# Attention's scores, products and exponentials in another order within a step

## The chip, the cores and the metric

The kernel runs on one NeuronCore of a Trainium2 chip. The time is that of one execution on the device, in microseconds (us). The kernel before took 920.6 us as the median of three runs (917.02 to 921.53).

Four engines matter here, each working through its own list of instructions in order: TensorE (PE, matrix products), ScalarE (ACT, tanh and exp), VectorE (DVE, sums, copies and transposes) and SyncE (SP, which issues most of the transfers). They wait for one another by semaphores. An instruction that waits holds up all that stand behind it on its engine.

## The reference

Softmax attention with capped scores comes first; its result feeds a layer of eight experts in which every expert takes 448 of the 3584 tokens.

```python
# q, k, v: (batch 8, heads 12, seq 448, head_dim 64), cap 30
scores = scale * np.matmul(q, k.transpose(0, 1, 3, 2))
scores = cap * np.tanh(scores / cap)
attn = np.exp(scores - scores.max(-1, keepdims=True))
attn = attn / (attn.sum(-1, keepdims=True) + 1e-09)
x = np.matmul(attn, v)          # then as 3584 tokens x 768
# logits = x @ w_gate; tokens go to experts in the order of their logits
out[mask] = np.maximum(x[mask] @ w1[e], 0) @ w2[e]
```

## The kernel before

Attention runs in 24 steps (the loop over `g`), three to a batch. I call the three m=0, m=1 and m=2, after the variable `m`. One step handles four heads.

**Scores.** Step g computes its scores in seven rounds, `qk(g,0)` to `qk(g,6)`. A round is four matmuls (64x64 weights, 448 columns) into a score tile `psS` of two PSUM banks, and then a tanh over 128x896 on ScalarE (line 145), which I call T0 to T6. Only two `psS` tiles exist, so the matmuls of a round wait until the tanh two rounds earlier has emptied its tile.

**Exponentials.** The seven rounds form groups: rounds 0 and 1, rounds 2 and 3, rounds 4 to 6. When a group's last tanh is issued, one exp over the whole group follows it on ScalarE (line 149): E0 and E1 over 128x1792, E2 over 128x2688. So ScalarE's list in a step is T0 T1 E0 T2 T3 E1 T4 T5 T6 E2.

**Products.** The exponentials of step g are multiplied with `v` one step later. `avq(g-1,j,x)` (line 177) is eight 64x64 matmuls that use rounds 2j and 2j+1 of the step before; j=3 uses round 6. They come as `x=0` with j=0 to 2 and as `x=1` with j=0 to 3, all into two `psA` tiles, which VectorE copies to `xT` (line 187) at the end of the step.

**Other work on TensorE** comes between `qk(g,1)` and the first products (place A), and between the x=0 and the x=1 part (place B). What stands there depends on m and on the batch. For batches 2 to 5 (steps 6 to 17): in m=0 two `xt` transposes at A and two at B (line 37); in m=1 two `xt` at A and sums and gates at B (`rnd`, line 194); in m=2 three lists of `rnd` at A and the transposes of the logits at B (line 209). Step 5, the m=2 step of batch 1, has the same `rnd` at A. From step 18 on A holds nothing in m=0, one list of `rnd` in m=1, the logit transposes in m=2.

**VectorE** adds the exponentials up into `es` (line 153), transposes the next step's `k` and `q` (line 125), and does the small work on logits. **SyncE** loads `k`, `q` and `v` up to three steps ahead.

The order on TensorE, ScalarE, VectorE and SyncE is the order in which the Python code issues the instructions; no planner changes it in this part. The rest of the kernel (routing, and the experts' two layers, some 580 us) follows attention and isn't touched.

Of the kernel before, what the change touches and what calls it, by code (L numbers as in the profile page):

```python
# [7 lines left out]
AF=mybir.ActivationFunctionType; ALU=mybir.AluOpType; AX=mybir.AxisListType  # L8
# [9 lines left out]
def attention(nc, tc, c1, xp, pM, q, k, v, cap, w_gate, xs, L1, ident, on_logits, on_turn, NDEF, xd, setup, mark):  # L18
# [33 lines left out]
    with ExitStack() as ctx:  # L52
# [11 lines left out]
        def load(g,part,lo=0,hi=HG,first=False):  # L64
            if g>=N: return
            b,m=divmod(g,NQ)
            h0=4*m
            if part==2:
                z=nat.tile([128,3,2*HG,D],F32,name="nv",bufs=5); zh=nat.tile([128,HG,D],F32,name="nvh",bufs=5)
                nats[g,2]=(z,zh)  # L70
                vv=v[b,h0:h0+4,0:384].rearrange("h (j p) d -> j p h d",j=3)
                for j in range(3): nc.sync.dma_start(z[:,j],vv[j])
                for o in range(2):
                    for t in range(2):
                        w=64*(1-o)
                        nc.sync.dma_start(zh[w:w+64,t],v[b,h0+2*t+o,384:448])
                return
            if lo==0: nats[g,part]=nat.tile([128,HG*NB,32],F32,name="kq"[part])
            z=nats[g,part]
            src=(k,q)[part]  # L80
            for t in range(2):
                for a in range(2):
                    w=(2*t+a)*32
                    (nc.scalar if first and a else nc.sync).dma_start(z[w:w+32,lo*NB:hi*NB,:],src[b,h0+2*t+lo:h0+2*t+hi,:,a*32:a*32+32].rearrange("h (k s) d -> s (h k) d",s=32))  # L84
# [6 lines left out]
        capt=c1.tile([128,1],F32,name="capt")  # L91
# [18 lines left out]
        def gates():  # L110
            for g in range(NQ):
                for t in range(2):
                    nc.sync.dma_start(wgs[t*64:t*64+64,2*g:2*g+2,:],w_gate[(4*g+2*t)*D:(4*g+2*t+2)*D].rearrange("(m d) e -> d m e",d=D))
            for bi,(g,p,hs) in enumerate(blk):
                for h in hs:
                    l=loc[h][1]; hp=slice(h%2*64,h%2*64+64)
                    nc.gpsimd.tensor_copy(gw[hp,bi,3+8*l:11+8*l],wgs[hp,h//2,:])
# [4 lines left out]
        def tr(g,part,lo=0,hi=HG):  # L122
            if g>=N: return
            if lo==0: tks[g,part]=tp.tile([128,HG,S],F32,name="t"+"kq"[part])
            nc.vector.transpose(tks[g,part].rearrange("p m s -> p (m s)")[:,lo*S:hi*S],nats[g,part][:,lo*NB:hi*NB,:].rearrange("p k d -> p (k d)"))
        GRP=((0,1),(2,3),(4,5,6)); LOC={r:(gi,n) for gi,rs in enumerate(GRP) for n,r in enumerate(rs)}
        def ev(g,r):
            gi,n=LOC[r]
            return eh[g,gi][:,n]
        ex=lambda g,o,j: ev(g,3*o+j if g==0 else 2*j+o)  # L130
        def qk(g,r):
            gi,n=LOC[r]
            if n==0: eh[g,gi]=ep.tile([128,len(GRP[gi]),2,S],F32,name=f"e{gi}")
            ps=pS.tile([128,2,512],F32,name="psS")
            if r<6:
                o,u=divmod(r,3) if g==0 else divmod(r,2)[::-1]
                for h in range(2):
                    hp=slice(h*64,h*64+64)
                    for c in range(2): nc.tensor.matmul(ps[c*64:c*64+64,h,:S],tks[g,0][hp,o,u*128+c*64:u*128+c*64+64],tks[g,1][hp,o,:],start=True,stop=True)  # L139
            else:  # L140
                for o in range(2):
                    for h in range(2):
                        hp=slice(h*64,h*64+64); w=64*(1-o)
                        nc.tensor.matmul(ps[w:w+64,h,:S],tks[g,0][hp,o,384:448],tks[g,1][hp,o,:],start=True,stop=True)  # L144
            nc.scalar.activation(ev(g,r),ps[:,:,:S],AF.Tanh,scale=s1)  # L145
            e=eh[g,gi]
            if g==N-1 and gi==2: e=ev(g,r)
            elif n<len(GRP[gi])-1: return
            nc.scalar.activation(e,e,AF.Exp,scale=capt,bias=bias)  # L149
        def esum(g,what):  # L150
            if not 0<=g<N: return
            if what=='e1': es_t[g]=es.tile([128,2,2,S],F32,name="es",bufs=5)
            t=es_t[g]; add=lambda o,a,b: nc.vector.tensor_tensor(o,a,b,op=ALU.add)  # L153
            if g==0 and what in ('e1','e2'):
                o=int(what[1])-1
                add(t[:,o],ex(g,o,0),ex(g,o,1)); add(t[:,o],t[:,o],ex(g,o,2))
                return
            if what=='e1': add(t,eh[g,0],eh[g,1])
            if what=='e2': add(t,t,eh[g,2][:,0:2])
            if what=='o1': add(t[:,0],t[:,0],ev(g,4))  # L160
            if what=='o2': add(t[:,1],t[:,1],ev(g,5))
            if what=='r':
                e=ev(g,6)
                for o in range(2):
                    w=slice(64*(1-o),128-64*o)
                    add(t[w,o],t[w,o],e[w])
        avp={}
        def avq(g,j,x):
            if not 0<=g<N: return
            if j==0 and x==0:  # L170
                for o in range(2): avp[g,o]=pT.tile([128,512],F32,name="psA")
            z,zh=nats[g,2]
            for w in range(2):
                o=w^x; hp=slice(w*64,w*64+64)
                for h in range(2):
                    lhs,rhs=(z[hp,j,HG*h+o,:],ex(g,o,j)) if j<3 else (zh[hp,h,:],ev(g,6))
                    nc.tensor.matmul(avp[g,o][h*64:h*64+64,:S],lhs,rhs[hp,h,:],start=(j==0 and x==0),stop=j==3)  # L177
# [5 lines left out]
        def av_out(g,o):  # L183
            if not 0<=g<N: return
            b,m=divmod(g,NQ)
            if m==0 and o==0: xT[b]=xp.tile([128,NP,S],F32,name="xT")
            nc.vector.tensor_copy(xT[b][:,2*m+o,:],avp[g,o][:,:S])  # L187
        def rnd(b,items,first,last):
            if first and b not in misc: misc[b]=pM.tile([128,512],F32,name="psM")
            ps=misc[b]  # L190
            for g,kind,a,c in items:
                if kind=='g': lhs=gw[:,a,:]; rhs=xT[b][:,c,:]
                else: lhs=ones[:,a,:]; rhs=es_t[b*NQ+c//4][:,c//2%2,c%2,:]
                nc.tensor.matmul(ps[g*32:g*32+32,:S],lhs,rhs,start=first,stop=last)  # L194
        lgs={}
        def spill(bb):
            if B-NDEF<=bb<B-2:
                spilled[bb]=xd[bb-(B-NDEF)]
                nc.sync.dma_start(spilled[bb],xT[bb])
        def logit_in(b):  # L200
            lgs[b]=xp.tile([128,S],F32,name="lg",bufs=1)
            nc.vector.tensor_copy(lgs[b],misc.pop(b)[:,:S])
# [36 lines left out]
        bias=c1.tile([128,1],F32,name="bias")  # L239
# [7 lines left out]
        for g in range(N):  # L247
            b,m=divmod(g,NQ); bb=b-1
            for z in LD.get(g,()): gates() if z=='g' else load(int(z[0]),int(z[1]))
            if g>2:  # L250
                load(g+1,2); load(g+3,0); load(g+3,1)
            last=g==N-1
            qk(g,0); qk(g,1)
            early=bb-1<B-NDEF
            if early and bb>0 and m<2:
                for p in ((0,1),(4,5))[m]: xt(bb-1,p)
            if m==2 and bb>=0:
                if early:
                    for r in (2,3,4): rnd(bb,R[r],False,r==4)
                else: logit(bb,0,3)  # L260
            if m==1 and not early: rnd(bb,R[2],False,False)
            for j in range(3): avq(g-1,j,0)
            tr(g+1,0)
            if m==2 and bb>=0 and early:
                logit_in(bb); spill(bb)
            for w in ('e2','r'): esum(g-1,w)
            qk(g,2); qk(g,3)
            if m==0:
                if early and bb>0: xt(bb-1,2); xt(bb-1,3)
                if not early: rnd(bb,R[0],True,False); rnd(bb,R[1],False,False)  # L270
                if bb>0: on_logits(bb-1)
            if m==1 and bb>=0:
                if early: rnd(bb,R[0],True,False); rnd(bb,R[1],False,False)
                else:
                    rnd(bb,R[3],False,False); rnd(bb,R[4],False,True)
                    logit_in(bb); spill(bb)
                if bb>0: on_turn(bb-1)
            if m==2 and bb>=0 and early: logit(bb,0,3)
            tr(g+1,1)
            qk(g,4); avq(g-1,0,1); avq(g-1,1,1)  # L280
            if last: av(g,0,0)
            qk(g,5); avq(g-1,2,1)
            qk(g,6); avq(g-1,3,1)
            esum(g,'e1')
            if g: av_out(g-1,0); av_out(g-1,1)
        g=N-1; b=B-1
# [657 lines left out]
```

## Time and profile before

| | |
|---|---|
| median of three runs | 920.6 us (917.02 to 921.53) |
| profiled execution | 920.02 us, its span 918.3 us |
| TensorE's mean granted clock | 0.986 of full speed |
| busy over the span | PE 879.2, DVE 608.9, ACT 582.3, POOL 350.4 us |

The span goes from the first to the last instruction of the trace; some 1.7 us of the execution lie around it. The busy time of an engine is a mean over stages with different limits: ScalarE is busy 63% of the whole span and over 90% of the attention steps. In the trace a line with "x16" stands for sixteen instructions merged; a round of scores or an `avq` shows as x8. A matmul's end is modelled and reaches into the next one, so lengths on TensorE are taken from start to start.

### The profile page before, as it was taken

How to read it: one execution, taken by the hardware profiler on the slowest of the kernel's cores; microseconds unless marked ns; L12 is line 12 of the kernel's file. 1: busy time of each engine (PE TensorE's matmuls, PEld its weight loads, DVE VectorE, ACT ScalarE, POOL GpSimd, SP SyncE). 2: the span in 40 equal slices, each digit the busy share in tenths (PEclk: the TensorE clock that was granted, in tenths of full speed). 3: DMA queues.
4: the chain of work that ended last, by engine and by line, in shares of the span. 5: the costliest groups of instructions: out<-in, count | busy, mean ns of one | idle time of the engine just before them, and what ended most of it. 6: DMA issues, size and time to landing. Idle time of an engine off the chain costs nothing.

```text
span 918.3 us, 17515 instructions
## 1 busy us (share of the span) xinstructions
PE 879.2 (96%) x6298; PEld 640.5 (70%) x6298; DVE 608.9 (66%) x2012; ACT 582.3 (63%) x836; POOL 350.4 (38%) x502
## 2 busy tenths in 40 slices
PE   7899999999999996799999999999999999999996
PEld 4333444434333344688889889989989899999996
DVE  3778888989788778776777776766767763231210
ACT  6999999999999947273482672762753742522520
POOL 7100000000000009482494393592682664753931
PEclk9999999999999999699999999999999999999998
DMA  8799999987992027661915516406407407327201
GB/s 121 115 133 133 149 153 171 132 166 140 186 170 50 1 75 227 200 197 37 316 44 165 190 43 218 150 29 232 148 18 249 147 15 269 113 70 257 70 10 51
DMA packets 291703, 123.07 MB, mean 134 GB/s; under 512 B 224768, under 2 KB 275712, under 8 KB 291104
## 3 DMA queue, kind: packets, MB, share of 16 engines
q1 hardware_dynamic: 285104, 99.70, 48.8%
q0 software_dynamic: 4656, 22.02, 6.7%
q8 instruction: 49, 0.80, 0.4%
q10 hardware_dynamic: 1856, 0.23, 0.2%
q14 instruction: 38, 0.31, 0.1%
HBM read 97.15 MB, written 24.77 MB: 133 GB/s over the span
## 4 chain that ended last, share of the span: by engine, by line
PE 70%; issue 9%; ACT 7%; DVE 6%; POOL 3%; DMA 2%; SPq 2%; POOLq 0%; DVEq 0%; ACTq 0%
PE psH L794 22%; PE psH L822 20%; PE psA L177 9%; PE psS L139 8%; ACT e L145 4%; PE psM L194 3%; ACT e L149 2%; PE psX L765 2%; PE psS L144 2%; SPq L84 2%; DVE cmpD L479 2%; DVE es L153 1%; DMA xg<-xs,idx 1%; POOL out_dram L807 1%; POOL w1l L726 1%
## 5 line engine op out<-in xcount | busy, mean ns | idle before, releaser
L822 PE MATMUL psH<-w2h,hh 128*128 128x384 f32 x896 | 249.0, 343 | 0.0
L822 PE MATMUL psH<-w2l,hh 128*128 128x384 f32 x512 | 174.6, 341 | 0.0
L145 ACT ACTIVATE e<-psS,s 128x896 f32<-128x896 f32 x168 | 160.5, 994 | 15.6 <-PE psS L144 8.1
L822 PEld LDWEIGHTS psH<-w2h,hh 128*128 128x128 f32 x896 | 162.7, 189 | 0.2
L149 ACT ACTIVATE e<-e,bias,capt 128x1792 f32<-128x1792 f32 (+2 forms) x74 | 154.3, 2085 | 2.5
L794 PE MATMUL psH<-xgh,w1h 128*128 128x448 f32 x384 | 143.1, 373 | 0.3 <-ACT xgh L770 0.3
L45 POOL TENSOR_TENSOR xn<-raw,rin 112x512 f32<-112x512 f32 x24 | 24.4, 1052 | 311.1 <-ACT raw L42 311.1
L794 PE MATMUL psH<-xgl,w1h 128*128 128x448 f32 x384 | 141.7, 369 | 0.0
L794 PE MATMUL psH<-xgh,w1l 128*128 128x448 f32 x384 | 141.2, 368 | 0.0
L139 PE MATMUL psS<-tq,tk 64*64 64x448 f32 x1152 | 130.8, 548 | 10.5 <-ACT e L145 10.2
L726 POOL TENSOR_TENSOR w1l<-w1r,w1h 128x768 fp32r<-128x768 f32 x62 | 114.1, 1840 | 21.8 <-ACT w1h L722 17.9
L726 POOL TENSOR_TENSOR w2l<-w2r,w2h 128x768 fp32r<-128x768 f32 x64 | 118.0, 1844 | 10.1 <-ACT w2h L722 10.0
L177 PE MATMUL psA<-e,nv 64*64 64x448 f32 x1104 | 120.1, 542 | 0.6 <-DVE xT L187 0.6
L153 DVE TENSOR_TENSOR es<-es,e 64x896 f32<-64x896 f32 (+2 forms) x74 | 100.5, 1359 | 4.9 <-ACT e L149 3.5
L828 ACT ACTIVATE on<-psH 128x384 f32<-128x384 f32 x48 | 23.6, 491 | 125.7 <-PE psH L822 124.9
L802 DVE SCALAR_TENSOR_TENSOR hh<-psH,hh 128x64 fp32r<-128x64 f32 (+1 forms) x128 | 44.1, 386 | 87.7 <-ACT hh L800 86.9
L139 PEld LDWEIGHTS psS<-tq,tk 64*64 64x64 f32 x1152 | 43.0, 133 | 78.3 <-ACT e L145 41.9
L822 PEld LDWEIGHTS psH<-w2l,hh 128*128 128x128 f32 x512 | 96.6, 189 | 0.0
L177 PEld LDWEIGHTS psA<-e,nv 64*64 64x64 f32 x1104 | 44.8, 133 | 60.7 <-issue 49.3
L800 ACT ACTIVATE hh<-psH 128x448 fp32r<-128x448 f32 x64 | 34.8, 543 | 69.8 <-PE psH L794 62.7
L794 PEld LDWEIGHTS psH<-xgh,w1h 128*128 128x128 f32 x384 | 72.5, 189 | 6.1 <-ACT xgh L770 0.5
L794 PEld LDWEIGHTS psH<-xgh,w1l 128*128 128x128 f32 x384 | 72.3, 188 | 5.7
(328 smaller groups left out, 1301.8 us busy)
## 6 DMA issues: line engine op xcount, KB each, us to landing
w1r<-in_moe_w_dram SPq DMA_DIRECT2D x64, 384.0 KB, 3.7
w2r<-in_moe_w_dram SPq DMA_DIRECT2D x32, 768.0 KB, 7.6
k<-in_k_dram SPq DMA_DIRECT2D x92, 112.0 KB, 3.5
q<-in_q_dram SPq DMA_DIRECT2D x92, 112.0 KB, 3.9
nv<-in_v_dram SPq DMA_DIRECT2D x72, 128.0 KB, 3.8
xs<-xn SPq DMA_DIRECT2D x4, 1344.0 KB, 7.3
xs<-xn SPq DMA_DIRECT2D x4, 896.0 KB, 5.2
xd<-xT SPq DMA_DIRECT2D x2, 1344.0 KB, 6.7
```

The lines of the kernel that those rows point to most:

```text
L45: (nc.gpsimd if late else nc.vector).tensor_tensor(xn[b][:,:,h0:h0+3:2,:],src, rin[b][:,:,slice(3*p,3*p+2) if p<4 else slice(6*p-22,6*p-18 ...
L139: for c in range(2): nc.tensor.matmul(ps[c*64:c*64+64,h,:S],tks[g,0][hp,o,u*128+c*64:u*128+c*64+64],tks[g,1][hp,o,:],start=True,stop=True)
L145: nc.scalar.activation(ev(g,r),ps[:,:,:S],AF.Tanh,scale=s1)
L149: nc.scalar.activation(e,e,AF.Exp,scale=capt,bias=bias)
L153: t=es_t[g]; add=lambda o,a,b: nc.vector.tensor_tensor(o,a,b,op=ALU.add)
L177: nc.tensor.matmul(avp[g,o][h*64:h*64+64,:S],lhs,rhs[hp,h,:],start=(j==0 and x==0),stop=j==3)
L194: nc.tensor.matmul(ps[g*32:g*32+32,:S],lhs,rhs,start=first,stop=last)
L726: (eng or nc.gpsimd).tensor_tensor(view(l),r,view(h).bitcast(F32),op=ALU.subtract)
L794: nc.tensor.matmul(ps[:,:C],a[:,c,:],b[:,c,:],start=(m==0),stop=(m==DC*3-1)); m+=1
L800: nc.scalar.activation(h[:,:C],ps[:,:C],AF.Relu)
L802: nc.vector.scalar_tensor_tensor(h[:,d:d+b-a],ps[:,a:b],0.0,h[:,a:b].bitcast(F32),op0=ALU.max,op1=ALU.subtract)
L822: nc.tensor.matmul(ps[:,:HD],h[:,f,a:a+128],spl[p,2,hf,f//2][w][:,f%2,:],start=(m==0),stop=(m==nm-1))
```

## The change

`qk` puts the exp of the first two groups on a list and issues it behind the next round's tanh. The step's order of scores and products changes with it.

```diff
+        wait=[]
         def qk(g,r):
...
             nc.scalar.activation(ev(g,r),ps[:,:,:S],AF.Tanh,scale=s1)
+            while wait: wait.pop(0)()
             e=eh[g,gi]
             if g==N-1 and gi==2: e=ev(g,r)
             elif n<len(GRP[gi])-1: return
-            nc.scalar.activation(e,e,AF.Exp,scale=capt,bias=bias)
+            act=lambda: nc.scalar.activation(e,e,AF.Exp,scale=capt,bias=bias)
+            if gi<2: wait.append(act)
+            else: act()
...
-            for j in range(3): avq(g-1,j,0)
+            for j in range(2): avq(g-1,j,0)
             tr(g+1,0)
...
-            qk(g,2); qk(g,3)
+            qk(g,2); avq(g-1,2,0); qk(g,3); qk(g,4)
             if m==0:
...
             tr(g+1,1)
-            qk(g,4); avq(g-1,0,1); avq(g-1,1,1)
+            qk(g,5)
+            avq(g-1,0,1); avq(g-1,1,1)
             if last: av(g,0,0)
-            qk(g,5); avq(g-1,2,1)
-            qk(g,6); avq(g-1,3,1)
+            qk(g,6)
+            avq(g-1,2,1); avq(g-1,3,1)
             esum(g,'e1')
```

On TensorE, in an m=2 step, from the `rnd` at place A on (the tiles `e_816`, `e_849` and `e_874` hold the three groups of exponentials of the step before), the kernel before has:

```order
L194 MATMUL psM<-xT,gw 32x448 x4
L177 MATMUL psA<-e_816,nv 64x448 x4
L177 MATMUL psA<-e_849,nv 64x448 x4
L177 MATMUL psA<-e_874,nv 64x448 x4
L139 MATMUL psS<-tq,tk 64x448 x8
L209 MATMUL psM<-ident,lg 112x128 x4
L139 MATMUL psS<-tq,tk 64x448 x4
L177 MATMUL psA<-e_816,nv 64x448 x4
L177 MATMUL psA<-e_849,nv 64x448 x4
L139 MATMUL psS<-tq,tk 64x448 x4
L177 MATMUL psA<-e_874,nv 64x448 x4
L144 MATMUL psS<-tq,tk 64x448 x4
```

In the changed kernel the same place reads as follows (the second and third group are now called `e_844` and `e_862`, and lines 139, 144, 177, 194 and 209 have become 140, 145, 181, 198 and 213).

```order
L198 MATMUL psM<-xT,gw 32x448 x4
L181 MATMUL psA<-e_816,nv 64x448 x4
L181 MATMUL psA<-e_844,nv 64x448 x4
L140 MATMUL psS<-tq,tk 64x448 x4
L181 MATMUL psA<-e_862,nv 64x448 x4
L140 MATMUL psS<-tq,tk 64x448 x8
L213 MATMUL psM<-ident,lg 112x128 x4
L140 MATMUL psS<-tq,tk 64x448 x4
L181 MATMUL psA<-e_816,nv 64x448 x4
L181 MATMUL psA<-e_844,nv 64x448 x4
L145 MATMUL psS<-tq,tk 64x448 x4
L181 MATMUL psA<-e_862,nv 64x448 x4
```

Round 2 moved ahead of the third product, round 4 ahead of the logit transposes, and rounds 5 and 6 moved one place forward against the products of the second part.

On ScalarE one step of the kernel before (the tanhs and exponentials that fill the same three groups) is:

```order
L145 ACTIVATE e_816<-psS,s_152 128x896 x2
L149 ACTIVATE e_816<-e_816,bias,capt 128x1792
L145 ACTIVATE e_849<-psS,s_152 128x896 x2
L149 ACTIVATE e_849<-e_849,bias,capt 128x1792
L145 ACTIVATE e_874<-psS,s_152 128x896 x3
L149 ACTIVATE e_874<-e_874,bias,capt 128x2688
```

and of the changed kernel:

```order
L146 ACTIVATE e_816<-psS,s_152 128x896 x2
L146 ACTIVATE e_844<-psS,s_152 128x896
L151 ACTIVATE e_816<-e_816,bias,capt 128x1792
L146 ACTIVATE e_844<-psS,s_152 128x896
L146 ACTIVATE e_862<-psS,s_152 128x896
L151 ACTIVATE e_844<-e_844,bias,capt 128x1792
L146 ACTIVATE e_862<-psS,s_152 128x896 x2
L151 ACTIVATE e_862<-e_862,bias,capt 128x2688
```

The list is now T0 T1 T2 E0 T3 T4 E1 T5 T6 E2. VectorE and SyncE keep their order.

## Rows read from the trace of the kernel before

**Rows 1.** Page's costliest groups: busy us, mean ns of one, idle before it and releaser.

```profile
L145 ACT ACTIVATE e<-psS,s 128x896 f32<-128x896 f32 x168 | 160.5, 994 | 15.6 <-PE psS L144 8.1
```

**Rows 2.** Stretches from one E2's start to another's: length, busy per engine, clock, DMA.

```profile
core 0: us, PE busy (x) PEld busy (x) DVE busy (x) ACT busy (x) POOL busy (x), PEclk, DMA share, GB/s
71.50:248.36 176.86, 176.12 (x1764) 74.76 (x1757) 155.00 (x227) 167.10 (x130) 0.00 (x0) 1.00 0.95 154
248.36:314.52 66.16, 64.15 (x651) 22.65 (x644) 54.16 (x83) 63.87 (x50) 0.00 (x0) 1.00 0.51 86
152.97:166.79 13.82, 13.82 (x147) 5.17 (x140) 11.71 (x14) 12.89 (x10) 0.00 (x0) 1.00 0.99 138
166.79:179.93 13.14, 12.95 (x135) 5.64 (x128) 12.20 (x30) 12.77 (x10) 0.00 (x0) 1.00 0.98 126
179.93:193.68 13.75, 13.75 (x144) 6.56 (x136) 11.86 (x12) 12.89 (x10) 0.00 (x0) 1.00 1.01 194
```

**Rows 3.** Timeline of TensorE, step 11 (m=2), then step 12: start, us, instruction.

```profile
152.43 1.68 PE L139 MATMUL psS<-tq,tk 64*64 64x448 f32 x16
154.04 0.96 PE L194 MATMUL psM<-xT,gw 128*32 128x448 f32 x8
...
156.43 2.49 PE L177 MATMUL psA<-e,nv 64*64 64x448 f32 x24
158.74 1.68 PE L139 MATMUL psS<-tq,tk 64*64 64x448 f32 x16
160.35 0.65 PE L209 MATMUL psM<-ident,lg 128*112 128x128 f32 x4
160.94 0.98 PE L139 MATMUL psS<-tq,tk 64*64 64x448 f32 x8
161.74 1.68 PE L177 MATMUL psA<-e,nv 64*64 64x448 f32 x16
163.24 0.93 PE L139 MATMUL psS<-tq,tk 64*64 64x448 f32 x8
...
166.25 1.68 PE L139 MATMUL psS<-tq,tk 64*64 64x448 f32 x16
167.86 1.09 PE L37 MATMUL psM<-ident,xT 128*112 128x128 f32 x8
168.88 2.49 PE L177 MATMUL psA<-e,nv 64*64 64x448 f32 x24
...
174.07 0.98 PE L139 MATMUL psS<-tq,tk 64*64 64x448 f32 x8 [0.19 <-ACT e L145]
```

**Rows 4.** Timeline of ScalarE, the end of step 11 and step 12.

```profile
159.74 1.91 ACT L145 ACTIVATE e<-psS,s 128x896 f32<-128x896 f32 x2 [0.43 <-PE psS L139]
...
166.79 2.63 ACT L149 ACTIVATE e<-e,bias,capt 128x2688 f32<-128x2688 f32 x1
169.33 1.89 ACT L145 ACTIVATE e<-psS,s 128x896 f32<-128x896 f32 x2
171.25 1.88 ACT L149 ACTIVATE e<-e,bias,capt 128x1792 f32<-128x1792 f32 x1
173.03 1.89 ACT L145 ACTIVATE e<-psS,s 128x896 f32<-128x896 f32 x2
174.95 1.88 ACT L149 ACTIVATE e<-e,bias,capt 128x1792 f32<-128x1792 f32 x1
176.74 1.89 ACT L145 ACTIVATE e<-psS,s 128x896 f32<-128x896 f32 x2
178.89 1.01 ACT L145 ACTIVATE e<-psS,s 128x896 f32<-128x896 f32 x1 [0.26 <-PE psS L144]
```

**Rows 5.** Timeline of TensorE, place A of a late m=1 step.

```profile
302.22 0.96 PE L194 MATMUL psM<-xT,gw 128*32 128x448 f32 x8
303.11 2.49 PE L177 MATMUL psA<-e,nv 64*64 64x448 f32 x24
```

**Rows 6.** Timeline of VectorE, the third transpose of `k`.

```profile
38.47 1.11 DVE L125 STREAM_TRANSPOSE tk<-k 128x896 f32<-128x896 f32 x1 [5.06 <-DMA k<-in_k_dram]
```

**Rows 7.** Timeline of TensorE, first products of step 3.

```profile
47.23 2.25 PE L177 MATMUL psA<-e,nv 64*64 64x448 f32 x18 [0.61 <-DVE xT L187]
```

## The prediction, made before the changed kernel ran

> **What bounds the kernel now.** I start from the page's row of the tanhs [rows 1]: 168 of them at 994 ns, and before them ScalarE sat idle for 15.6 us in all, most of it waiting for scores. That is the most that ScalarE alone could give back. Whether it can be had depends on TensorE, so I next cut the attention steps into stretches from one E2 to the next [rows 2]. In the batches with much work beside attention, ScalarE is busy 12.89 of 13.82 us in the m=2 step and TensorE 13.82 of 13.82; in m=1 it is 12.89 against 13.75 of 13.75; in m=0 12.77 against 12.95 of 13.14. The granted clock is 1.00 throughout, the upper of the two levels (2.4 GHz), so nothing here is a slow clock. The engines are so evenly loaded that TensorE sets the length of m=1 and m=2, and ScalarE, with a wait at its last tanh, that of m=0. From step 18 on (248.36 to 314.52) TensorE is busy 64.15 of 66.16 and has room.
>
> The third view is the order of time on both engines. TensorE in step 11 [rows 3] starts one group behind the other without a hole: rounds 0 and 1 from 152.43, the `rnd` at A from 154.04, three products from 156.43, rounds 2 and 3 from 158.74. A group of scores or products takes 0.75 us from start to start (four groups, round 5 to the last product, from 163.24 to 166.25). ScalarE in step 12 [rows 4] shows what one tanh or exp costs in its place: a pair of tanhs takes 1.89, so the second starts 0.90 after the first; the exp that needs the second starts only when that has ended (169.33 + 1.89 = 171.22, exp at 171.25); the tanh behind an exp starts 1.78 after it (171.25 to 173.03), before the exp's 1.88 are over. The third tanh in a row comes 2.15 after the first (176.74 to 178.89) instead of 1.79, because its scores could only start when the first had emptied its tile.
>
> **The change part by part.** No arithmetic is added or removed; the time changes by waits alone.
>
> *The exponentials moved.* E0 and E1 now stand behind a tanh that they don't need. No row shows an exp in such a place. The nearest from one side is a tanh behind a tanh, 0.90 after it; from the other an exp behind its own tanh, 1.03 (0.99 and the 0.04 up to the exp). I take 0.89 to 0.90, since every neighbour that doesn't depend on the one before overlaps its end, exp and tanh included. That saves 0.14 twice a step. It could gain no more than that, and lose nothing against 1.03.
>
> The Trainium skill says, in "ScalarE: Activation LUTs", section "What ACT_TABLE_LOAD costs", that back-to-back activations overlap by about 93 ns. The trace agrees where they are independent (0.99 against 0.90) and not where the exp reads the tanh's result (171.22, then 171.25); by the rule taken for every pair, the move would save nothing, and a ScalarE-bound step would stay at 13.14.
>
> The shortest step that ScalarE then allows: T0 to T2 2.15 (three tanhs in a row stand at the start now instead of the end, with the same two score tiles, so the 0.26 idle moves with them), T2 to E0 0.89, E0 to T3 1.78, T3 to E1 twice 0.89, E1 to T5 1.79, T5 to T6 0.89, T6 to E2 1.04 (178.89 to 179.93), E2 to T0 2.54 (166.79 to 169.33) [rows 2, 4]. The sum is 12.86, against 13.14.
>
> *The third tanh brought forward.* T2 used to have E0 between itself and T1, so its scores could come late. Now ScalarE wants it right behind T1. But on TensorE round 2 still stands behind place A and two products. That makes a new chain. From the end of T3, which frees the tile for round 5: 0.05 to the first matmul (173.03 + 0.99, then 174.07); round 5 0.80 (160.94 to 161.74, the price after a wait); two products 1.50; round 6 and two products 2.26 (three groups); rounds 0 and 1 of the next step 1.61; place A; two products 1.56 (156.43 to 158.74 less one group); from round 2's first matmul to T2 1.00 (158.74 to 159.74); T2 to E0 0.89; E0 to T3 1.78; T3 itself 0.99. Together 12.44 plus what stands at A [rows 3, 4]. All other waits on that way are met earlier: round 6 needs T4, which ends 0.9 after T3 while round 6 comes 2.35 after; rounds 0 and 1 need T5 and T6, which end 3.6 and 4.5 after T3 while these rounds come 4.6 and 5.4 after.
>
> - m=2, A is 2.39 (154.04 to 156.43): 14.83, against 13.82. TensorE, which had no hole, now waits before round 5 for T3, about 1.2 us, and no cover is left for it.
> - m=0 and m=1, A is 1.02 (167.86 to 168.88): 13.46, against 13.14 and 13.75.
> - A empty: 12.44, so ScalarE's 12.86 holds.
> - late m=1, A is 0.89 [rows 5]: 13.33. Late m=2, A is the logit transposes, 0.59 (160.35 to 160.94): 13.03.
>
> *The sum.* Steps 5 to 17 are five of m=2 and four each of the others: 5 x 14.83 + 8 x 13.46 = 181.83, against 176.86 [rows 2]: +4.97. Steps 18 to 22: 12.86 + 13.33 + 13.03 + 12.86 + 13.33 = 65.41, against 66.16: -0.75. Steps 0 to 4 would win 0.28 each, but not all of it. The third transpose of `k` waits until 38.47 for its transfer [rows 6], in a part where the loads are issued as fast as SyncE can; behind it on VectorE stands all that leads to the copies for which the first products of step 3 wait at 47.23 [rows 7]. So T2 of step 3 can't come before 47.23 + 1.56 + 1.00 = 49.79; from there E2 comes 0.89 + 1.78 + 5.50 later (T3 to E2 by the floor's terms), at 57.96, and the next E2 at 57.96 + 12.86 = 70.82, against 71.50 (where the first stretch of rows 2 begins): -0.68. The last step ends in another order; I cost it at nothing, between -0.3 and +0.5. All that follows attention starts as much later. 4.97 - 0.75 - 0.68 = +3.5 us.
>
> The profiled execution took 920.02 us, so 923.5 by its own clock; it stands 0.6 below the median of 920.6. I say 924.0, which is 3.4 (0.4%) above that median.
>
> **The rivals.**
>
> *A: an exp behind a foreign tanh starts no earlier than behind its own* (1.03). Then the floor is 13.14 again and the chain 12.58 plus A. Steps 5 to 17 become 183.65 (+6.79), steps 18 to 22 13.14 + 13.47 + 13.17 + 13.14 + 13.47 = 66.39 (+0.23), the start 58.10 + 13.14 = 71.24 (-0.26): +6.8, or 927. For it speaks that no row shows the case; against it that the tanh behind an exp overlaps, so a change of function needs no empty pipeline. It is decided by one distance, T2 to E0.
>
> *B: TensorE's holes go and nothing takes their place.* If round 2 came in time somehow, each step would take the longer of ScalarE's 12.86 and TensorE's busy time: 13.82, 12.95 and 13.75 [rows 2]. Steps 5 to 17 then give 5 x 13.82 + 4 x 12.95 + 4 x 13.75 = 175.9 (-1.0), steps 18 to 22 64.3 (-1.9), the start -0.7: -3.6, or 917. Against it stands the order itself: round 2 is behind A and two products, and 154.04 to 158.74 less one group is 3.95, more than the pair of tanhs covers.
>
> *C: TensorE has far more room than its rows say.* "Perfetto Trace Analysis" of the Trainium skill, section "Identifying the Most-Contended Engine", warns that matmul busy time tells little and that the busy share of weight loads is the better measure; that is 5.17 of 13.82 in the m=2 step, 37%. Worked out from rows, a TensorE with room would let ScalarE's 12.86 hold in all of steps 5 to 22: 18 x 12.86 = 231.5 against 243.0, with the start -12.2 us, or 908. Against it: the starts in [rows 3] follow one another by 0.75 a group from 163.24 to 166.25, whatever waits, and that pace is the same where ScalarE isn't awaited.
>
> *D: a slower collision that I haven't priced at its full size*, above all in VectorE's list, whose copies release the product tiles; its steps are busy 11.7 to 12.2 us [rows 2]. At 0.3 us more in each of steps 5 to 17 it would be 3.9 more, some 928.
>
> **How the numbers follow.** Within 0.5% is what a measurement of this kernel can tell from no change: 4.6 us, 916.0 to 925.2. My forecast has a chance of 0.60 with its own range of 921.5 to 926.5; of that 0.17 lies above 925.2. Rival A 0.14 and D 0.12 are all slower. B has 0.09, of which 0.02 is faster; C 0.05, all faster. So faster 0.07, same 0.50, slower 0.43. The range reaches from 919.5, which leaves out C and most of B, to 928.5, which leaves out only the far end of A and D.
>
> **What would show it.** In the changed profile, the idle before T2 is worth looking at first: by the terms above T1 ends 9.93 after T3 of the step before, and T2 starts 9.77 plus A after it, so 2.2 us in an m=2 step, 0.9 where two `xt` stand at A, and 0.3 where A is empty (there T0's tile decides). TensorE waits for ScalarE before round 5, some 1.2 us in m=2. E2 to E2 reads 14.8, 13.5 and 13.5 in a batch, and 12.9 in the steps without work at A. From T2 to E0 0.89 is right and 1.03 is rival A. The last tanh no longer waits. I am wrong if the m=2 step stays near 13.8, or if an idle time grows that isn't before T2 or round 5.

## The result and the profile after

The changed kernel takes 924.71 us (median of ten runs, 921.99 to 925.77), against 920.56 (ten runs, 917.02 to 923.42) for the kernel before. The ratio is 1.0041, with a 95% interval of 1.0027 to 1.0054: slower by 0.4%, within the 0.5% that I had called "no change", and 0.7 us above the 924.0 that I had forecast. The profiled execution has a span of 923.5 us, against 918.3.

The page's row of the tanhs, which had 15.6 us of idle time [rows 1], now reads (columns as there):

```profile
L146 ACT ACTIVATE e<-psS,s 128x896 f32<-128x896 f32 x168 | 160.7, 1001 | 28.4 <-PE psS L140 28.4
```

All of the 28.4 us before a tanh are now waits for scores of line 140, that is rounds 0 to 5; the wait before the last tanh (line 144 before, 145 now) is gone. The same stretches as in [rows 2], from one E2's start to another's:

```profile
71.55:253.85 182.30, 175.44 (x1761) 70.57 (x1757) 156.12 (x227) 163.23 (x131) 0.00 (x0) 1.00 0.91 150
253.85:319.24 65.39, 63.46 (x648) 23.23 (x644) 54.16 (x83) 62.76 (x50) 0.00 (x0) 1.00 0.47 86
155.18:170.06 14.88, 13.93 (x144) 5.17 (x140) 11.92 (x14) 12.55 (x11) 0.00 (x0) 1.00 0.95 127
170.06:183.53 13.47, 12.95 (x132) 5.80 (x128) 12.32 (x31) 12.55 (x11) 0.00 (x0) 1.00 0.94 128
183.53:197.00 13.47, 13.47 (x140) 5.35 (x136) 11.74 (x11) 12.55 (x11) 0.00 (x0) 1.00 0.78 180
```

Steps 5 to 17 take 182.30 us instead of 176.86, steps 18 to 22 65.39 instead of 66.16. The m=2 step is 1.06 longer, and TensorE, which had no hole in it, now stands idle for 0.95 of its 14.88; ScalarE's busy time fell from 12.89 to 12.55 and its step grew all the same. The clock is 1.00 as before.

Where ScalarE waits is seen in its timeline of step 11 (m=2) and the start of step 12, as in [rows 4]:

```profile
155.18 2.63 ACT L151 ACTIVATE e<-e,bias,capt 128x2688 f32<-128x2688 f32 x1
157.71 1.88 ACT L146 ACTIVATE e<-psS,s 128x896 f32<-128x896 f32 x2
161.89 1.01 ACT L146 ACTIVATE e<-psS,s 128x896 f32<-128x896 f32 x1 [2.30 <-PE psS L140]
162.80 1.87 ACT L151 ACTIVATE e<-e,bias,capt 128x1792 f32<-128x1792 f32 x1
164.57 1.89 ACT L146 ACTIVATE e<-psS,s 128x896 f32<-128x896 f32 x2
166.35 1.88 ACT L151 ACTIVATE e<-e,bias,capt 128x1792 f32<-128x1792 f32 x1
168.12 1.90 ACT L146 ACTIVATE e<-psS,s 128x896 f32<-128x896 f32 x2
170.06 2.63 ACT L151 ACTIVATE e<-e,bias,capt 128x2688 f32<-128x2688 f32 x1
```

The one wait is 2.30 us before T2 (161.89); behind it E0 starts 0.91 after T2 (162.80), and nothing waits any more up to E2. TensorE in the same step, as in [rows 3]:

```profile
155.33 1.68 PE L140 MATMUL psS<-tq,tk 64*64 64x448 f32 x16
156.95 0.96 PE L198 MATMUL psM<-xT,gw 128*32 128x448 f32 x8
...
159.34 1.74 PE L181 MATMUL psA<-e,nv 64*64 64x448 f32 x16
160.89 0.93 PE L140 MATMUL psS<-tq,tk 64*64 64x448 f32 x8
...
164.01 0.65 PE L213 MATMUL psM<-ident,lg 128*112 128x128 f32 x4
165.62 0.98 PE L140 MATMUL psS<-tq,tk 64*64 64x448 f32 x8 [0.95 <-ACT e L146]
```

Round 2 starts at 160.89, behind `rnd` (156.95) and two products (159.34); T2 follows 1.00 later. Round 5 at 165.62 waits for T3, 1.61 after the start of the logit transposes that themselves take 0.59. That is the chain of the prediction.

### The profile page after: what moved, and what is told of

Read it like the earlier page. It is cut to its first block, busy times and chain, and to the rows that moved or that the text cites. A ratio compares the mean times of both kernels' runs of the same rounds, so it can differ in the third digit from the quotient of the medians.

```text
span 923.5 us, 17494 instructions
## 1 busy us (share of the span) xinstructions
PE 875.7 (95%) x6298; PEld 636.3 (69%) x6298; DVE 614.8 (67%) x2012; ACT 575.6 (62%) x836; POOL 347.7 (38%) x502
## 4 chain that ended last, share of the span: by engine, by line
PE 70%; issue 9%; ACT 6%; DVE 5%; SPq 3%; POOL 3%; DMA 2%; POOLq 0%; DVEq 0%; ACTq 0%
PE psH L799 21%; PE psH L827 20%; PE psA L181 10%; PE psS L140 8%; ACT e L146 4%; PE psM L198 4%; SPq L84 2%; PE psX L770 2%; DVE cmpD L484 2%; DMA xg<-xs,idx 2%; PE psS L145 1%; ACT e L151 1%; PE psM L37 1%; POOL out_dram L812 1%; POOL w1l L731 1%
## 5 line engine op out<-in xcount | busy, mean ns | idle before, releaser
L146 ACT ACTIVATE e<-psS,s 128x896 f32<-128x896 f32 x168 | 160.7, 1001 | 28.4 <-PE psS L140 28.4
L181 PE MATMUL psA<-e,nv 64*64 64x448 f32 x1104 | 122.6, 540 | 0.4 <-DVE xT L191 0.4
L181 PEld LDWEIGHTS psA<-e,nv 64*64 64x64 f32 x1104 | 42.0, 133 | 61.4 <-issue 55.4
```

## The experiments

My theory: T2 is now wanted right behind T1, but its scores stand behind place A and the products, so each step's length is a chain through T2, E0 and T3. The first rival says that the moved scores and products cost the time by themselves; others name VectorE, or hold that TensorE has room. The ratios are against the kernel before as measured along with each experiment (23 runs, median 920.77 for the first four, 920.34 for the others). All lengths are from one E2's start to the next in steps 11, 12 and 13 (m=2, m=0, m=1), where the kernel before has 13.82, 13.14 and 13.75 and the changed one 14.88, 13.47 and 13.47.

**The exponentials alone.** The changed kernel with the old order of scores and products:

```diff
-            for j in range(2): avq(g-1,j,0)
+            for j in range(3): avq(g-1,j,0)
-            qk(g,2); avq(g-1,2,0); qk(g,3); qk(g,4)
+            qk(g,2); qk(g,3)
-            qk(g,5)
-            avq(g-1,0,1); avq(g-1,1,1)
+            qk(g,4); avq(g-1,0,1); avq(g-1,1,1)
-            qk(g,6)
-            avq(g-1,2,1); avq(g-1,3,1)
+            qk(g,5); avq(g-1,2,1)
+            qk(g,6); avq(g-1,3,1)
```

> The exponentials alone: E0 behind T2 and E1 behind T4, the order of scores and products as in the kernel before. My theory (T2 is wanted right behind T1 but its scores stand behind place A and the products): the loss comes with the exponentials already, since round 2 now stands behind three products. The chain runs from T3 over T4, E1 and T5, whose end frees the tile for round 0, then rounds 0 and 1, A, three products, round 2: 12.20 plus A, so m=2 steps of 14.6, m=0 13.3, m=1 13.5; steps with empty A 12.8. In all some +2 to +3 us against before, 923. Rival (the moved scores and products are what costs, the exponentials only win their 0.14 twice a step): m=2 stays at 13.8 or less, every other step is shorter, and the time falls below before, to 916 to 918.

Measured: 924.99 us, ratio 1.0041 (1.0025 to 1.0058). The steps (stretches as above):

```profile
155.89:170.76 14.87, 14.50 (x144) 4.95 (x140) 11.73 (x14) 12.56 (x10) 0.00 (x0) 1.00 0.84 117
170.76:184.19 13.43, 13.26 (x132) 5.57 (x128) 12.99 (x31) 12.56 (x10) 0.00 (x0) 1.00 0.95 123
184.19:197.61 13.42, 13.42 (x140) 5.24 (x136) 10.99 (x11) 12.56 (x10) 0.00 (x0) 1.00 0.81 183
```

The whole loss is there with the exponentials alone, so the rival falls. My chain for it was 0.3 too short in m=2: I had let it end with the wait of round 0 for T5, while in TensorE's timeline of this run round 1 also waits, for T6, so rounds 0 and 1 took 1.81 from start to start instead of 1.61 (that is 0.2 of the 0.3; the rest I can't place):

```profile
169.89 1.88 PE L140 MATMUL psS<-tq,tk 64*64 64x448 f32 x16 [0.32 <-ACT e L146]
171.70 1.09 PE L37 MATMUL psM<-ident,xT 128*112 128x128 f32 x8
```

So the length is about the same with either order, but the chain isn't: with the old order it closes over round 0, with the new one over round 5.

**The order alone.** The changed order of scores and products, each exp where it stood before:

```diff
-            if gi<2: wait.append(act)
-            else: act()
+            act()
```

> The order of scores and products alone, the exponentials where the kernel before has them. Theory: the two parts need each other. With E0 right behind T1, T2 has more time, but rounds 4 and 5 now stand ahead of products and wait longer for T2 and T3: m=2 about 14.3, m=0 13.5, m=1 14.1, and even steps with an empty A up to 14; in all some 6 to 11 us above before, 927 to 931. Rival (the order of TensorE doesn't matter, only ScalarE's list): the time is that of before, 920.

Measured: 930.55 us, ratio 1.0103 (1.0085 to 1.0121), steps of 14.24, 13.56 and 14.18. Here even the late steps grow: steps 18 to 22 take 69.82. ScalarE in step 18 shows why:

```profile
262.30 1.89 ACT L146 ACTIVATE e<-psS,s 128x896 f32<-128x896 f32 x2
264.22 1.88 ACT L151 ACTIVATE e<-e,bias,capt 128x1792 f32<-128x1792 f32 x1
266.00 1.95 ACT L146 ACTIVATE e<-psS,s 128x896 f32<-128x896 f32 x2
269.20 1.01 ACT L146 ACTIVATE e<-psS,s 128x896 f32<-128x896 f32 x1 [1.25 <-PE psS L145]
```

The last tanh (269.20) waits 1.25 for round 6, which stands behind B, round 5 and two products; ahead of them, in TensorE's timeline of this run, round 4 waits 1.22 for T2, which now comes behind E0. The two halves of the change do belong together: the new order costs 9.8 us with the old exponentials (930.55 against 920.77) and nothing with the new ones (924.71 with it, 924.99 without, each 4.2 above the kernel before that was measured along with it).

**Round 2 earlier in the m=2 steps.** This takes the two products out of the chain and leaves all else:

```diff
-            for j in range(2): avq(g-1,j,0)
+            nk=0 if m==2 and bb>=0 and early else 2
+            for j in range(nk): avq(g-1,j,0)
+            qk(g,2)
+            for j in range(nk,2): avq(g-1,j,0)
...
-            qk(g,2); avq(g-1,2,0); qk(g,3); qk(g,4)
+            avq(g-1,2,0); qk(g,3); qk(g,4)
```

> The changed kernel, but in the m=2 steps with `rnd` at place A round 2 comes right behind A, ahead of the two products. Theory: the chain over T2 loses the two products there (12.44 - 1.56 + 2.39 = 13.3), so TensorE's own work decides, 13.8; m=0 and m=1 stay at 13.5. Five such steps lose 1.1 each: 5.5 us less than the changed kernel, 919. Rival (the m=2 step is long because of VectorE or the products' tiles, not because of T2's place): m=2 stays near 14.9 and the time near 924.7.

Measured: 920.08 us, ratio 0.9986 (0.9974 to 0.9997). The three steps:

```profile
153.47:167.23 13.76, 13.76 (x144) 5.17 (x140) 11.31 (x14) 12.71 (x10) 0.00 (x0) 1.00 1.00 149
167.23:180.79 13.56, 13.04 (x135) 5.79 (x128) 12.72 (x31) 12.56 (x10) 0.00 (x0) 1.00 1.02 137
180.79:194.26 13.47, 13.47 (x140) 5.34 (x136) 11.73 (x11) 12.55 (x10) 0.00 (x0) 1.00 0.82 185
```

The m=2 step lost 1.12 us, TensorE has no hole again (busy 13.76 of 13.76), and the wait before T2 fell from 2.30 to 0.79:

```profile
156.01 1.88 ACT L146 ACTIVATE e<-psS,s 128x896 f32<-128x896 f32 x2
158.68 1.01 ACT L146 ACTIVATE e<-psS,s 128x896 f32<-128x896 f32 x1 [0.79 <-PE psS L140]
```

Moving one round of scores past two products, in five of the 24 steps, gave back all that the change had cost. VectorE's list is the same in this version, so it wasn't the cause of the m=2 step's length.

**Round 2 as early as A allows, everywhere.**

```diff
-            nk=0 if m==2 and bb>=0 and early else 2
+            nk=2
+            if m==2 and bb>=0 and early: nk=0
+            elif early and bb>0 or m>0 and not early: nk=1
```

> As the run before, and where A holds less (two `xt`, one list of `rnd`, the logit transposes) round 2 stands behind one product instead of two. Theory: in these steps the chain falls by 0.75 to 12.7 (m=0) and 12.6 (late m=1), below what ScalarE or TensorE needs alone: m=0 12.9 to 13.1, m=1 13.5 to 13.7, m=2 13.8, late steps 12.8 to 13.0. About 40.3 a batch against 40.7 before and 41.8 changed; in all 917 to 918. Rival (T2's place decides in m=2 alone): no difference from the run before, 919.

Measured: 918.59 us, ratio 0.9970 (0.9954 to 0.9987), the first version that is clearly below before (the interval of the one ahead of it ends at 0.9997).

```profile
71.75:248.54 176.79, 176.37 (x1761) 75.82 (x1757) 154.72 (x227) 164.71 (x130) 0.00 (x0) 1.00 0.90 154
248.54:313.89 65.35, 64.16 (x651) 23.13 (x644) 54.67 (x83) 62.99 (x50) 0.00 (x0) 1.00 0.51 90
153.16:166.98 13.82, 13.82 (x147) 5.17 (x140) 11.07 (x13) 12.71 (x10) 0.00 (x0) 1.00 0.94 140
166.98:179.86 12.88, 12.88 (x135) 5.53 (x124) 12.04 (x30) 12.62 (x10) 0.00 (x0) 1.00 0.98 139
179.86:193.86 14.00, 13.91 (x142) 6.93 (x140) 12.64 (x12) 12.66 (x10) 0.00 (x0) 1.00 0.78 177
```

I had expected 40.3 for a batch; it is 13.82 + 12.88 + 14.00 = 40.70, the 40.71 of before: m=0 became shorter, and m=1 longer by as much. TensorE is busy in all but 0.09 us of it, but that isn't all its own work. A wait that is shorter than the modelled end of the matmul before it stands in the busy column as work: the same matmuls of a batch sum to 40.61 here and to 40.35 in the changed kernel, where m=1 takes 13.47. In this trace's m=1 step TensorE waits for VectorE twice:

```profile
179.32 0.93 PE L181 MATMUL psA<-e,nvh 64*64 64x448 f32 x8
180.34 1.73 PE L140 MATMUL psS<-tq,tk 64*64 64x448 f32 x16
...
183.01 1.17 PE L181 MATMUL psA<-e,nv 64*64 64x448 f32 x8
```

```profile
179.09 1.10 DVE L125 STREAM_TRANSPOSE tq<-q 128x896 f32<-128x896 f32 x1
...
182.02 1.14 DVE L191 COPY xT<-psA 128x448 f32<-128x448 f32 x2
```

Round 0 starts 1.02 behind a product that takes 0.75, and 0.15 after the transpose of its `q` ends (179.09 + 1.10). The first product starts at 183.01, but half of its matmuls only when the second copy out of `psA` ends (182.02 + 1.14); behind it rounds 3 and 4 take 1.80 from start to start (186.07 to 187.87) instead of 1.61. Together that is 0.46 of the 0.53 by which this m=1 step exceeds 13.47. With m=0 down to 12.88 VectorE no longer has its list done in time (in the run before, with m=0 at 13.56, the same transpose ended 0.47 ahead of round 0); that is read from the traces, and no run tested another order on VectorE. In the late steps my expectation failed too: steps 18 to 22 take 65.35, as in the changed kernel (65.39), since m=1 stays at 13.48 there.

In the attention steps this trace is only 0.6 us ahead of before (E2 of step 22 at 313.89 against 314.52); the rest of the 2 us between the medians I can't place in the traces.

**More work at A, and the same at B.** One `xt` of the m=0 steps does its transposes twice, first the one at A, then one at B (the output is the same):

```diff
-        for j in range(NJ):
+        for j in list(range(NJ))*rep:
             nc.tensor.transpose(ps[:CP,j*128:(j+1)*128],xT[b][:,p,j*CP:(j+1)*CP],ident)
...
-                for p in ((0,1),(4,5))[m]: xt(bb-1,p)
+                for p in ((0,1),(4,5))[m]: xt(bb-1,p,rep=2 if p==0 else 1)
```

For B, `xt(bb-1,2)` gets `rep=2` in place of the last line.

> The changed kernel with one of the two `xt` at place A of the m=0 steps of batches 2 to 5 done twice (the same transposes into the same tile, 0.51 us more of TensorE work). Theory: A is part of the chain from T3 to T2, so these four steps grow by all of it, 13.47 to 13.98, although TensorE stands idle for 0.6 us before round 5 in the same step. Rival (TensorE has room, as its share of weight loads would have it, or the length of m=0 comes from VectorE): 13.5 as before.

> The same 0.51 us of double work, but in an `xt` at place B of the same steps. Theory: B lies in the time in which TensorE waits for T3 before round 5 (0.6 us), so it costs nothing: 13.5, and the wait before round 5 shrinks to about 0.1. Rival (any work on TensorE costs its time): 13.98.

The m=0 step with the double work at A:

```profile
171.13:185.03 13.90, 13.38 (x136) 6.22 (x132) 12.31 (x31) 12.55 (x10) 0.00 (x0) 1.00 0.95 120
```

and at B:

```profile
170.18:183.65 13.47, 13.38 (x136) 6.23 (x132) 12.32 (x31) 12.55 (x11) 0.00 (x0) 1.00 0.72 108
```

TensorE's busy time grew by 0.43 in both (from 12.95 to 13.38; I had taken 0.51). At A the step grew by the same 0.43, at B by nothing; all of steps 5 to 17, with four such steps, take 184.04 and 182.30, against 182.30 in the changed kernel. (The times, one run each: 926.94 and 924.76.) So the chain runs through A and not through B: in these steps the same work on TensorE costs time or not by its place.

**The start.** The version with round 2 early, and the gates' six small loads issued later:

```diff
-        LD={0:['10','11','02','20','21'],1:['12','g','30','31','22'],2:['40','41','32','50','51']}
+        LD={0:['10','11','02','20','21'],1:['12','30','31','g','22'],2:['40','41','32','50','51']}
```

> The version with round 2 as early as A allows, and the six small loads of the gates' weights issued behind the fourth step's `k` and `q` instead of ahead of them (SyncE spends 3.9 us on them). Theory on the start: the third transpose of `k` then comes some 3 us earlier, the copies for step 3's first products too, T2 of step 3 no longer waits (its distance from T1 falls from 2.2 to 1.2), and steps 0 to 4 keep their 0.3 each: about 1 us less than the version without, 917.5. Rival (the start is bound by something else, the transfers' bandwidth above all): step 3 stays at 13.5 to 13.8.

Measured: 918.73 us, ratio 0.9978 (0.9964 to 0.9993), no different from the version without; I had expected 917.5. Step 3 lost its wait, as expected (12.78 long instead of 13.80), and step 4 got one (13.53 instead of 12.79). VectorE's transposes of `k` that waited for their transfers:

```profile
35.21 1.11 DVE L125 STREAM_TRANSPOSE tk<-k 128x896 f32<-128x896 f32 x1 [1.19 <-DMA k<-in_k_dram]
...
51.29 1.11 DVE L125 STREAM_TRANSPOSE tk<-k 128x896 f32<-128x896 f32 x1 [4.73 <-DMA k<-in_k_dram]
```

The third one ran at 35.21 instead of 38.47 [rows 6], the next at 51.29, 2.8 later than the 48.47 of before. E2 of step 4 started at 71.27, against 71.50 before and 71.75 without this edit. In the next run, with the same start, T2 waits in step 1 instead (1.33 us), and E2 of step 4 starts at 71.26. So some step waits for its loads with either order of issue; what limits the loads themselves no run shows.

**One list of `rnd` from m=1 to m=0 in the late steps.**

```diff
-            if m==1 and not early: rnd(bb,R[2],False,False)
...
-            elif early and bb>0 or m>0 and not early: nk=1
+            elif early and bb>0 or m>1 and not early: nk=1
...
-                if not early: rnd(bb,R[0],True,False); rnd(bb,R[1],False,False)
+                if not early: rnd(bb,R[0],True,False); rnd(bb,R[1],False,False); rnd(bb,R[2],False,False)
```

With nothing left at A, round 2 stands behind two products again in the late m=1 steps (the second pair of lines).

> As the run before, and from step 18 on the list of `rnd` at place A of m=1 goes to place B of m=0. Theory: TensorE has room in m=0 there (12.2 of 12.8) and not in m=1, where the last tanh waits behind its products: m=1 13.5 to 12.8, m=0 12.8 to 13.1, 0.8 us less in all, 917. Rival (the late m=1 step is long for another reason than A): 13.5 still, and m=0 longer, so 0.6 us more.

Measured: 918.30 us, ratio 0.9972 (0.9957 to 0.9987). Steps 18 and 19 (m=0 and m=1):

```profile
248.06:261.54 13.48, 13.47 (x143) 5.16 (x136) 11.93 (x27) 12.66 (x10) 0.00 (x0) 1.00 0.99 138
261.54:274.33 12.79, 12.68 (x136) 4.69 (x128) 9.75 (x9) 12.55 (x10) 0.00 (x0) 1.00 0.90 195
```

My expectation failed by half: m=1 fell to 12.79, but m=0 rose to 13.48, not 13.1. Its busy column reads 13.47, and again a wait hides in it:

```profile
249.78 1.85 PE L181 MATMUL psA<-e,nv 64*64 64x448 f32 x16
251.64 0.98 PE L140 MATMUL psS<-tq,tk 64*64 64x448 f32 x8
```

Round 2 starts 1.86 behind two products that take 1.50, 0.05 after T0 has ended (250.60 + 0.99 in ScalarE's timeline) and emptied its tile; from there on TensorE runs without a hole to the end of the step, B included. I had counted TensorE's room over the whole step (12.2 of 12.8), but part of it lies in this wait of 0.36 ahead of round 2, where the list at B can't use it. Nothing was won over the two versions before it: the three stand at 918.30 to 918.73, all some 0.25% below the kernel before and not to be told apart.

## Why the prediction was right

- *The chain over T2.* Forecast 14.83 for m=2 and 13.46 for m=0 and m=1; measured 14.88, 13.47, 13.47. The waits before T2, forecast as 2.2, 0.9 and 0.3 (A empty), are 2.30, 0.89 and 0.20 in the trace. Before round 5 of m=2 I had put 1.2; the trace has 0.95, and the terms of the chain themselves give 1.0. Late m=1 and m=2 make the 65.39 of steps 18 to 22 with the floor, forecast 65.41. The runs with round 2 moved and with more work at A show the cause: take the two products out of the chain and m=2 returns to 13.76, add 0.43 at A and the step grows by 0.43.
- *The floor of ScalarE.* Forecast 12.86; with A empty the steps take 12.79 (step 4 of the changed kernel, 58.76 to 71.55; 261.54 to 274.33 above). The third tanh came a little earlier than its model in [rows 4].
- *The exp behind a foreign tanh.* Taken as 0.89 to 0.90, measured 0.91 (161.89 to 162.80). Rival A, which needed 1.03, falls. (Its own start counted one such exp where there are two: 58.24 and not 58.10.) The overlap that the Trainium skill states in "ScalarE: Activation LUTs", section "What ACT_TABLE_LOAD costs", holds for this pair too: 0.10 here (1.01 less 0.91).
- *TensorE's room.* Rival C falls: the steps didn't come down to 12.86, and with round 2 moved the m=2 step's weight loads are busy 5.17 of 13.76 us while the engine's matmuls follow one another without a hole. Rival B fails for the changed kernel; with round 2 early everywhere, its 12.95 for m=0 was met (12.88), its sum for steps 5 to 17 was not (176.79 against 175.9), since m=1 took 14.00. D didn't show in the changed kernel: by the trace no matmul and no activation of its steps 11 to 13 waits for VectorE. It does show once T2's waits are cut, in that m=1 step.
- *The start, mis-sized.* This is the term that was most off: forecast -0.68 up to E2 of step 4, measured +0.05 (71.55 against 71.50). I had counted from T2 of step 3, which I put at 49.79; it came at 50.60, and E2 of step 4 followed 20.95 later, forecast 21.03. The first products of step 3 started 0.31 later than before (47.54 against 47.23 [rows 7]). T2 came 3.06 behind them and not 1.56 + 1.00: these products go into two `psA` tiles, and I had waited for one copy only. The second ends at 48.02 (46.89 + 1.13), so half of the products start 0.5 later, and round 2, from 49.10 on, comes in pieces among them.

```profile
46.89 1.13 DVE L191 COPY xT<-psA 128x448 f32<-128x448 f32 x2
```

```profile
47.54 1.88 PE L181 MATMUL psA<-e,nv 64*64 64x448 f32 x14 [0.43 <-DVE xT L191]
```

```profile
50.60 1.01 ACT L146 ACTIVATE e<-psS,s 128x896 f32<-128x896 f32 x1 [0.87 <-PE psS L140]
```

  Step 1 waited as well, which I hadn't forecast: its `q` landed late, and its T2 waited 1.25 us. That isn't what set the end of the stretch: in two other runs with the same order in steps 0 to 4 (round 2 early everywhere; double work at A) T2 of step 1 waited 0.20, T2 of step 3 came at 50.79 and 50.80, and E2 of step 4 at 71.75.

- *The sum.* +4.97, -0.75 and -0.68 were forecast; the traces show +5.44 (182.30 - 176.86), -0.77 and +0.05, and 0.48 more between E2 of step 22 and the end (604.26 against 603.78). That is 5.2 between the two profiled spans. In steps 5 to 17 the m=2 step is 0.05 longer than forecast and the others 0.01, which makes 0.33 of the 0.47 there. The medians differ by 4.15 only, since the profiled execution before lay 0.5 below its median and the one after 0.6 above. Against the +3.5 forecast the traces show +5.2, so that the median came within 0.7 us of 924.0 is in part luck; that the step lengths did is not. From E2 of step 22 to the end the traces of other versions vary by more than 0.48 (918.0 - 313.89 = 604.11 in one, 916.6 - 313.42 = 603.18 in another), so I don't read that part.

## What to carry to other kernels

When two engines hand work to and fro through two buffers, write down the closed chain that one buffer makes, with every instruction that stands in between on either engine; its sum is the step's length if it exceeds the work of both engines. Count TensorE's work from start to start: the busy column takes short waits for work (40.61 and 40.35 for the same matmuls). An instruction moved forward on one engine needs its input moved forward on the other, past everything that stands there, or the wait only changes its place. Work on TensorE cost time by its place: 0.43 us inside the chain cost 0.43, and in the hole behind it nothing. A new order can also make another engine the one that is late: here VectorE, once TensorE's step had become shorter.

## What I had not expected of the hardware

Little of the hardware, more of its records. I had taken TensorE's waits in the batch steps of the kernel before for time that a better order would win back, and put the batch at 40.3 us. With the waits before T2 cut it still took 40.70. The busy column, 40.52 of 40.71 before (13.82 + 12.95 + 13.75) and then 40.61 of 40.70, looks as if TensorE's work filled it; the best length that each step had in any of these traces, 13.76, 12.88 and 13.47, sums to 40.11. Most of the difference (0.46) went into waits for VectorE that the column hides. Whether one order can have all three lengths at once no run shows.
